# The product g of a step placed behind the selection of the step in front of it, on VectorE, in the second half of the first MLP layer

## The chip, the core and the metric

The kernel runs on one core of a Trainium2 chip. The metric is the device time of one execution in microseconds (us). Three runs of the kernel before took 456.14, 456.65 and 458.29 us; the median is 456.65. The profile was taken in one further execution of 458.42 us, whose instructions span 456.7 us.

## What is computed

Three things in a row, on 1536 tokens (2 batches of 768): a gated linear attention with 8 heads of 40 columns, then two MLP layers of 320 -> 2048 -> 320. Only the first layer is touched. Cut to what matters:

```python
def _moe_ref(x, w_in, w_out):          # first layer
    h = x @ w_in                       # (1536, 320) @ (320, 2048)
    g = h - np.tanh(h)
    return (g @ w_out).astype(np.float32)
def _moe2_ref(x, w_in, w_out):         # second layer
    h = x @ w_in
    sp = np.where(h > 20.0, h, np.log1p(np.exp(np.minimum(h, 20.0))))
    return ((h * np.tanh(sp)) @ w_out).astype(np.float32)
```

## The kernel before

The weights of a layer come in NF = 16 chunks of 128 hidden columns. Numbers are carried in two parts, a rounded high part and the rest, so that TensorE multiplies high by high, high by low and low by high.

**Steps.** The first layer cuts the tokens into NB = 6 blocks of 256. A step is one block with NP = 2 chunks. Each block is visited twice: a first pass over its first chunks (8 for block 0, 10 for the others; `CUT`), and a second pass over the rest. All first passes come first: steps 0 to 28. Then the second passes: steps 29 to 32 for block 0, and three steps for each further block, up to step 47. The last block's first pass begins with step 24. From step 48 on it is the second layer, one chunk with 512 tokens to a step.

**One step.** `mm1(i)` makes h in PSUM: 16 matmuls of 256 columns (line 579). `tile1(i)` makes g = h - tanh(h) so that it stays exact near zero, by a product and a selection:

```python
nc.scalar.activation(out=u, in_=h, func=AF.Tanh, scale=G_B)            # L601 ACT
nc.scalar.activation(out=t, in_=h, func=AF.Tanh)                       # L602 ACT
squared[:] = [nc.scalar.activation(out=u, in_=u, func=AF.Square, ...)] # L603 ACT
mark[:] = [nc.vector.tensor_tensor(g, in0=u, in1=h, op=ALU.mult)]      # L606 DVE, the product
nc.vector.tensor_tensor(t, in0=h, in1=t, op=ALU.subtract)              # L607 DVE, the difference
relus[i] = nc.scalar.activation(out=u, in_=u, func=AF.Relu, ...)       # L608 ACT, the mask
nc.vector.copy_predicated(out=g, mask=u.bitcast(U32), data=t)          # L610 DVE, the selection
```

`split_g` rounds g to gh on ScalarE (L590) and takes the rest gl on GpSimd (L591). `mm2`, LAG = 2 steps behind in the program's text, adds gh and gl times the output weights to two accumulators in PSUM (L642 to L644, 12 matmuls of 320 columns). After a block's last step VectorE adds the two accumulators into xo, four instructions (L659).

**What limits a step's start.** h has three PSUM buffers, so the matmuls of step i + 3 wait until step i's last reader of h is done, which is the difference L607. u, t and g have two buffers each. The accumulators have two, one pair of tiles at a time: a block's first L642 waits for the L659 of the block in front.

**What else these engines do there.** Weights of the second layer are converted a chunk at a time: DVE L202, ACT L210, DVE L214, ACT L217, DVE L220 and L221, six chunks in steps 29 to 47. The second layer's transposed input is made from finished blocks: PE L288, ACT L290, DVE L293.

**What sets the order.** The program is recorded with a scheduler that plays it through on a timeline and puts each engine's instructions in the order in which they come up there; the engines then run their lists strictly in that order and wait at semaphores. `after([x])` adds an edge behind x for instructions of x's own engine: it sets the order in the list and no semaphore. Since the scheduler plays the whole program, one such edge can move instructions on other engines as well.

Of the kernel before, what the change touches and what calls it, by code (L numbers as in the profile page):

```python
# [10 lines left out]
U32 = mybir.dt.uint32  # L11
# [14 lines left out]
def kernel(  # L26
# [11 lines left out]
    nc = tc.nc  # L38
# [19 lines left out]
    NP = 2  # L58
# [22 lines left out]
    NB = len(blocks1)  # L81
# [47 lines left out]

    texp, tbl, dls, squared = [], [], [], []  # L130

    scored, gated, rounded, relus, slots = {}, {}, {}, {}, {}

    spq, cvd, hold = [], [], []

# [8 lines left out]
    def after(x):  # L144
        e = ExitStack()
        for i in x:
            e.enter_context(tc.issue_after(i.ins))
        return e
# [409 lines left out]
    segs = [(bi, 0, CUT[bi]) for bi in range(NB)] + [(bi, CUT[bi], NF) for bi in range(NB)]  # L558
    tiles = [(0, bi, f) for bi, f0, f1 in segs for f in range(f0, f1, NP)]
    half = len(tiles)  # L560
    tiles += [(1, bi, f) for s in supers for f in range(NF) for bi in s]
    hps, gs, accs = {}, {}, {}

    def span(i):
        l, bi, f = tiles[i]
        return l, bi, range(f, f + (1 if l else NP)), len(blk[l, bi]) * L
# [21 lines left out]
    def split_g(i, g, n):  # L588
        gh, gl = (gp.tile([P, MX], F32R, tag=t, name=t)[:, 0:n] for t in ("gh", "gl"))
        rounded[i] = nc.scalar.activation(out=gh, in_=g, func=AF.Copy)  # L590
        nc.gpsimd.tensor_tensor(gl, in0=g, in1=gh.bitcast(F32), op=ALU.subtract)  # L591
        gs[i] = (gh, gl)

    def tile1(i):
        l, bi, fs, nt = span(i)
        n = len(fs) * nt
        h = hps.pop(i)
        u, t, g = (g2.tile([P, MX], F32, tag=nm, name=nm)[:, 0:n] for nm in "utg")

        with after([scaled[0, fs[-1] + 1]] if i < CUT[0] // NP - 1 else []):  # L600
            nc.scalar.activation(out=u, in_=h, func=AF.Tanh, scale=G_B)  # L601
            nc.scalar.activation(out=t, in_=h, func=AF.Tanh)  # L602
        squared[:] = [nc.scalar.activation(out=u, in_=u, func=AF.Square, scale=G_SA)]  # L603
        joint = i == CUT[0] // NP - 1
        with after([gated[NP]] if joint else []):
            mark[:] = [nc.vector.tensor_tensor(g, in0=u, in1=h, op=ALU.mult)]  # L606
        nc.vector.tensor_tensor(t, in0=h, in1=t, op=ALU.subtract)  # L607
        relus[i] = nc.scalar.activation(out=u, in_=u, func=AF.Relu, bias=bias[:, 0:1])  # L608
        with after([gated[NP + 1]] if joint else []):
            nc.vector.copy_predicated(out=g, mask=u.bitcast(U32), data=t)  # L610
        split_g(i, g, n)


# [62 lines left out]
    def program():  # L676
# [183 lines left out]
        for i in range(len(tiles)):  # L860
# [29 lines left out]
            if l == 0:  # L890
                tile1(i)
                if 1 < i < 4:
                    session(2 * i - 3, 2 * i - 1 + (i > 2), i == 3, [cvd[0], relus[2]] if i < 3 else [rounded[2]] * 3)
                qm.append(i)
                if len(qm) > LAG:
                    mm2(qm.pop(0))
                if i:
                    ahead(min(int(14 * (k + (i - i0 + 1) / n_seg + 0.4)), (8, 14)[i - 1] if i < 3 else 14 * NB))
                if k >= T2:
                    next(sg, None)  # L900
                    next(sg, None)
            else:
                tile2(i)
                qm.append(i)
                if len(qm) > LAG2:
                    mm2(qm.pop(0))
                next(sg, None)
# [66 lines left out]
```

## Time and profile before

| | before |
|---|---|
| median of 3 runs | 456.65 us |
| profiled execution, its own time | 458.42 us |
| its span (first to last instruction) | 456.7 us |
| PE busy | 439.7 us (96%) |
| DVE, ACT, POOL busy | 295.4, 284.2, 98.7 us |
| granted TensorE clock, mean | 1.000 |

How to read it: PE is TensorE, DVE VectorE, ACT ScalarE, POOL GpSimd. PE is busy nearly all the time, so the time of the kernel is the sum of PE's work and of the stretches in which PE stands. Matmuls overlap their neighbours in the profile (a row of 0.31 us is followed by the next after 0.15), so the distance from start to start tells more than the busy time. In a timeline row the square brackets give the time that the engine stood idle before it, and what it waited for. Steps can be found in the timeline by counting L606: step 24 is at 179.31 us, step 47 at 275.11.

### The profile page before, as it was taken

How to read it: one execution, taken by the hardware profiler on the slowest of the kernel's cores; microseconds unless marked ns; L12 is line 12 of the kernel's file. 1: busy time of each engine (PE TensorE's matmuls, PEld its weight loads, DVE VectorE, ACT ScalarE, POOL GpSimd, SP SyncE). 2: the span in 40 equal slices, each digit the busy share in tenths (PEclk: the TensorE clock that was granted, in tenths of full speed). 3: DMA queues.
4: the chain of work that ended last, by engine and by line, in shares of the span. 5: the costliest groups of instructions: out<-in, count | busy, mean ns of one | idle time of the engine just before them, and what ended most of it. 6: DMA issues, size and time to landing. Idle time of an engine off the chain costs nothing.

```text
span 456.7 us, 7966 instructions
## 1 busy us (share of the span) xinstructions
PE 439.7 (96%) x3116; PEld 399.4 (87%) x3116; DVE 295.4 (65%) x520; ACT 284.2 (62%) x519; POOL 98.7 (22%) x103
## 2 busy tenths in 40 slices
PE   9899999899999999999988899999999999999997
PEld 5657889899899999999987888998889899889996
DVE  7899999977989985566775865986922212211112
ACT  6687996584866858988687767675643332322331
POOL 2307153353442521433242232000000000000000
PEclk9999999999999999999999999999999999999999
DMA  8985526222343210001111120343110000010001
GB/s 253 377 297 184 173 76 217 76 99 69 100 161 104 65 65 1 0 17 50 63 65 65 63 64 1 86 166 130 63 59 0 1 1 1 11 48 0 1 0 57
DMA packets 22728, 38.03 MB, mean 83 GB/s; under 512 B 1348, under 2 KB 17028, under 8 KB 22692
## 3 DMA queue, kind: packets, MB, share of 16 engines
q1 hardware_dynamic: 22692, 37.54, 25.2%
q8 instruction: 24, 0.39, 0.3%
q14 instruction: 12, 0.10, 0.1%
HBM read 35.41 MB, written 1.97 MB: 82 GB/s over the span
## 4 chain that ended last, share of the span: by engine, by line
PE 52%; DVE 20%; issue 12%; ACT 7%; POOL 5%; DMA 3%; POOLq 0%; ACTq 0%; DVEq 0%; SPq 0%
PE h L579 22%; PE acc L644 7%; PE acc L642 7%; PE acc L643 7%; POOL gl L591 5%; DMA raw<-in_w_dram 3%; DVE g L606 3%; PE pv L409 2%; DVE t L607 2%; DVE raw L214 2%; DVE w L220 2%; PE sc L385 2%; PE w_ps L683 2%; DVE g L610 2%; DVE raw L202 2%
## 5 line engine op out<-in xcount | busy, mean ns | idle before, releaser
L579 PE MATMUL h<-xT,w 128*128 128x256 f32 (+1 forms) x1152 | 203.7, 321 | 6.5 <-DVE t L607 4.7
L579 PEld LDWEIGHTS h<-xT,w 128*128 128x128 f32 x1152 | 166.6, 188 | 22.9 <-PE acc L644 2.4
L642 PE MATMUL acc<-w,gh 128*128 128x320 f32 x384 | 119.3, 313 | 0.3 <-ACT xo L662 0.2
L643 PE MATMUL acc<-w,gh 128*128 128x320 f32 x384 | 118.4, 310 | 0.0
L644 PE MATMUL acc<-w,gl 128*128 128x320 f32 x384 | 113.5, 312 | 1.6 <-POOL gl L591 1.6
L591 POOL TENSOR_TENSOR gl<-g,gh 128x512 fp32r<-128x512 f32 x48 | 64.7, 1348 | 141.3 <-ACT gh L590 134.9
L623 DVE TENSOR_TENSOR gl<-g,gh 128x512 fp32r<-128x512 f32 x48 | 33.1, 690 | 82.5 <-ACT g L622 82.4
L621 ACT ACTIVATE gh<-h 128x512 fp32r<-128x512 f32 x48 | 28.8, 599 | 78.4 <-PE h L579 76.8
L642 PEld LDWEIGHTS acc<-w,gh 128*128 128x128 f32 x384 | 72.2, 188 | 3.0 <-ACT gh L590 0.5
L643 PEld LDWEIGHTS acc<-w,gh 128*128 128x128 f32 x384 | 72.2, 188 | 2.2
L644 PEld LDWEIGHTS acc<-w,gl 128*128 128x128 f32 x384 | 70.4, 188 | 4.0 <-POOL gl L591 2.9
L606 DVE TENSOR_TENSOR g<-u,h 128x512 f32<-128x512 f32 x48 | 32.8, 683 | 32.5 <-POOL gl L591 14.9
L608 ACT ACTIVATE u<-u,bias 128x512 f32<-128x512 f32 x48 | 34.8, 727 | 16.4 <-DVE g L606 16.3
L590 ACT ACTIVATE gh<-g 128x512 fp32r<-128x512 f32 x48 | 30.5, 634 | 20.0 <-DVE g L610 19.9
L610 DVE COPY_PREDICATED g<-u,t 128x512 f32<-128x512 uint32 x48 | 36.3, 780 | 2.4 <-ACT u L608 2.3
L217 ACT ACTIVATE w<-raw 128x704 fp32r<-128x704 f32 x32 | 27.3, 859 | 14.6 <-DVE raw L214 14.4
L607 DVE TENSOR_TENSOR t<-h,t 128x512 f32<-128x512 f32 x48 | 32.7, 682 | 0.0
L601 ACT ACTIVATE u<-h 128x512 f32<-128x512 f32 x48 | 28.4, 592 | 4.6 <-PE h L579 4.6
L214 DVE SCALAR_TENSOR_TENSOR raw<-raw 128x704 uint32<-128x704 uint32 x32 | 30.8, 966 | 0.7 <-ACT raw L207 0.3
L603 ACT ACTIVATE u<-u 128x512 f32<-128x512 f32 x48 | 30.3, 644 | 0.0
L602 ACT ACTIVATE t<-h 128x512 f32<-128x512 f32 x48 | 28.7, 598 | 0.0
L622 ACT ACTIVATE g<-h 128x512 f32<-128x512 f32 x48 | 28.5, 594 | 0.0
(106 smaller groups left out, 436.2 us busy)
## 6 DMA issues: line engine op xcount, KB each, us to landing
raw<-in_w_dram SPq DMA_DIRECT2D x32, 704.0 KB
qk_t<-in_qk_dram SPq DMA_DIRECT2D x12, 512.0 KB
kv_t<-in_kv_dram SPq DMA_DIRECT2D x12, 324.0 KB
out_dram<-xo SPq DMA_DIRECT2D x12, 160.0 KB
xo<-in_og_dram SPq DMA_DIRECT2D x2, 800.0 KB
xo<-in_og_dram SPq DMA_DIRECT2D x1, 320.0 KB
sd<-nr SPq DMA_DIRECT2D x20, 4.0 KB
md<-nr SPq DMA_DIRECT2D x10, 8.0 KB
```

Of the source, the lines that this page charges most:

```text
L214: third[layer, f] = nc.vector.scalar_tensor_tensor(z, in0=z, scalar=3, in1=lo32, op0=ALU.logical_shift_left, op1=ALU.bitwise_or)
L579: y = nc.tensor.matmul(t[:, k * nt:(k + 1) * nt], lhsT=w[:, o:o + P], rhs=x[:, kk, :], start=(n == 0), stop=(n == len(pairs) - 1),)
L590: rounded[i] = nc.scalar.activation(out=gh, in_=g, func=AF.Copy)
L591: nc.gpsimd.tensor_tensor(gl, in0=g, in1=gh.bitcast(F32), op=ALU.subtract)
L606: mark[:] = [nc.vector.tensor_tensor(g, in0=u, in1=h, op=ALU.mult)]
L607: nc.vector.tensor_tensor(t, in0=h, in1=t, op=ALU.subtract)
L608: relus[i] = nc.scalar.activation(out=u, in_=u, func=AF.Relu, bias=bias[:, 0:1])
L610: nc.vector.copy_predicated(out=g, mask=u.bitcast(U32), data=t)
L623: mark.append(nc.vector.tensor_tensor(gl, in0=g, in1=gh.bitcast(F32), op=ALU.subtract))
L642: turn(lambda: nc.tensor.matmul(a, lhsT=gh[:, sl], rhs=wh, start=(f in ends_), stop=False))
L643: turn(lambda: nc.tensor.matmul(a, lhsT=gh[:, sl], rhs=wl, start=False, stop=False))
L644: turn(lambda: nc.tensor.matmul(a, lhsT=gl[:, sl], rhs=wh, start=False, stop=end))
```

## The change

`chosen[i]` keeps the selection of step i. For every step after `STEADY` = 24 (steps 25 to 47) the product L606 gets an edge behind the selection of the step in front. Both are on VectorE. No instruction is added or taken away, and no semaphore.

```diff
-    scored, gated, rounded, relus, slots = {}, {}, {}, {}, {}
+    scored, gated, rounded, relus, slots, chosen = {}, {}, {}, {}, {}, {}
...
+    STEADY = tiles.index((0, NB - 1, 0))
...
-        with after([gated[NP]] if joint else []):
+        with after([gated[NP]] if joint else [chosen[i - 1]] if i > STEADY else []):
             mark[:] = [nc.vector.tensor_tensor(g, in0=u, in1=h, op=ALU.mult)]
...
-            nc.vector.copy_predicated(out=g, mask=u.bitcast(U32), data=t)
+            chosen[i] = nc.vector.copy_predicated(out=g, mask=u.bitcast(U32), data=t)
```

Lines behind the new one have numbers one higher in the kernel after: L606 is L607 there, and so on.

VectorE, before, from the product of step 41 to the difference of step 43 (raw and w are weights of the second layer):

```order
340 L606 TENSOR_TENSOR g<-u,h 128x512
341 L607 TENSOR_TENSOR t<-h,t 128x512
342 L202 TENSOR_SCALAR raw<-raw 128x704
343 L606 TENSOR_TENSOR g<-u,h 128x512
344 L607 TENSOR_TENSOR t<-h,t 128x512
345 L610 COPY_PREDICATED g<-u,t 128x512
346 L214 SCALAR_TENSOR_TENSOR raw<-raw 128x704
347 L610 COPY_PREDICATED g<-u,t 128x512
348 L220 TENSOR_TENSOR w<-raw,w 128x576
349 L221 TENSOR_TENSOR w<-raw,w 64x128
350 L606 TENSOR_TENSOR g<-u,h 128x512
351 L607 TENSOR_TENSOR t<-h,t 128x512
```

VectorE, after, from the product of step 41 to the difference of step 43:

```order
349 L607 TENSOR_TENSOR g<-u,h 128x512
350 L608 TENSOR_TENSOR t<-h,t 128x512
351 L202 TENSOR_SCALAR raw<-raw 128x704
352 L214 SCALAR_TENSOR_TENSOR raw<-raw 128x704
353 L611 COPY_PREDICATED g<-u,t 128x512
354 L607 TENSOR_TENSOR g<-u,h 128x512
355 L608 TENSOR_TENSOR t<-h,t 128x512
356 L220 TENSOR_TENSOR w<-raw,w 128x576
357 L221 TENSOR_TENSOR w<-raw,w 64x128
358 L611 COPY_PREDICATED g<-u,t 128x512
359 L607 TENSOR_TENSOR g<-u,h 128x512
360 L608 TENSOR_TENSOR t<-h,t 128x512
```

Two steps went through together before (two products, then two selections); now one step's selection is followed by the next step's product, and L220 and L221, which stood in front of a pair's first product, stand behind a difference and in front of a selection.

ScalarE, before, from the squares of steps 41 and 42 on (L608 masks, L590 rounding, L601 and L602 the tanh of step 43, L217 the rounding of a weight chunk):

```order
319 L603 ACTIVATE u<-u 128x512 x2
320 L608 ACTIVATE u<-u,bias 128x512 x2
321 L590 ACTIVATE gh<-g 128x512
322 L601 ACTIVATE u<-h 128x512
323 L602 ACTIVATE t<-h 128x512
324 L217 ACTIVATE w<-raw 128x704
325 L603 ACTIVATE u<-u 128x512
326 L590 ACTIVATE gh<-g 128x512
```

ScalarE, after, from the mask of step 41 on:

```order
331 L609 ACTIVATE u<-u,bias 128x512
332 L604 ACTIVATE u<-u 128x512
333 L217 ACTIVATE w<-raw 128x704
334 L591 ACTIVATE gh<-g 128x512
335 L602 ACTIVATE u<-h 128x512
336 L603 ACTIVATE t<-h 128x512
337 L609 ACTIVATE u<-u,bias 128x512
338 L604 ACTIVATE u<-u 128x512
```

ScalarE's list repeats with one step now: mask, square of the next step, (a weight chunk,) rounding, the two tanh of the step after that. L217 stood behind the tanh of the pair and in front of its square, and now stands between a square and a rounding.

PE, before, the matmuls for h of steps 34 and 35 and the first six accumulating ones of step 31 (one row is one matmul where no count stands):

```order
627 L579 MATMUL h<-xT,w 128x256 x32
628 L642 MATMUL acc<-w,gh 128x320
629 L643 MATMUL acc<-w,gh 128x320
630 L642 MATMUL acc<-w,gh 128x320
631 L643 MATMUL acc<-w,gh 128x320
632 L644 MATMUL acc<-w,gl 128x320 x2
```

PE, after, from the rest of step 35's matmuls on, with eleven of step 32's accumulating matmuls and the first six of step 36:

```order
645 L580 MATMUL h<-xT,w 128x256 x9
646 L643 MATMUL acc<-w,gh 128x320
647 L644 MATMUL acc<-w,gh 128x320
648 L643 MATMUL acc<-w,gh 128x320
649 L644 MATMUL acc<-w,gh 128x320
650 L580 MATMUL h<-xT,w 128x256 x6
651 L645 MATMUL acc<-w,gl 128x320 x2
652 L643 MATMUL acc<-w,gh 128x320
653 L644 MATMUL acc<-w,gh 128x320
654 L645 MATMUL acc<-w,gl 128x320
655 L643 MATMUL acc<-w,gh 128x320
656 L644 MATMUL acc<-w,gh 128x320
```

Before, 32 matmuls of two steps alternate with 24 accumulating ones; now the two kinds alternate step by step, and some of the next step's h are put between the gh and the gl part of a step. POOL's and SP's lists keep their order.

## Rows read from the trace of the kernel before

**Rows 1.** Busy us of each engine by stretch of us, with instructions and TensorE's clock
```profile
199.00:217.00 18.00, 18.00 (x139) 18.00 (x139) 11.89 (x21) 14.98 (x29) 5.60 (x4) 1.00 0.13 41
225.00:252.00 27.00, 23.43 (x173) 22.00 (x172) 19.06 (x38) 20.21 (x36) 8.25 (x6) 1.00 0.17 55
```

**Rows 2.** Groups by line on PE, 225.1 to 282: busy, mean ns | idle, releaser
```profile
L579 PE MATMUL h<-xT,w 128*128 128x256 f32 x160 | 20.8, 284 | 4.2 <-DVE t L607 4.2
...
L644 PE MATMUL acc<-w,gl 128*128 128x320 f32 x53 | 15.0, 317 | 1.0 <-POOL gl L591 1.0
```

**Rows 3.** Timeline of PE: start, us, engine line, xcount [idle before]
```profile
202.69 3.89 PE L579 MATMUL h<-xT,w 128*128 128x256 f32 x32
...
217.22 3.91 PE L579 MATMUL h<-xT,w 128*128 128x256 f32 x32
220.96 0.82 PE L288 MATMUL xt<-ident,xo 128*128 128x128 f32 x6
221.54 0.39 PE L642 MATMUL acc<-w,gh 128*128 128x320 f32 x1
...
259.91 2.15 PE L579 MATMUL h<-xT,w 128*128 128x256 f32 x16 [0.95 <-DVE t L607]
...
269.10 3.82 PE L579 MATMUL h<-xT,w 128*128 128x512 f32 x16
...
277.44 2.01 PE L579 MATMUL h<-xT,w 128*128 128x512 f32 x8
```

**Rows 4.** Timeline of DVE in front of the PE wait at 259.91
```profile
257.38 0.76 DVE L220 TENSOR_TENSOR w<-raw,w 128x576 fp32r<-128x576 f32 x1 [1.03 <-ACT w L217]
...
258.48 0.69 DVE L606 TENSOR_TENSOR g<-u,h 128x512 f32<-128x512 f32 x1
259.08 0.69 DVE L607 TENSOR_TENSOR t<-h,t 128x512 f32<-128x512 f32 x1
```

**Rows 5.** Timeline of ACT: one wait for h, one L217, and steps 46 and 47
```profile
197.50 0.60 ACT L601 ACTIVATE u<-h 128x512 f32<-128x512 f32 x1 [0.26 <-PE h L579]
...
256.50 0.85 ACT L217 ACTIVATE w<-raw 128x704 fp32r<-128x704 f32 x1
...
272.36 0.63 ACT L590 ACTIVATE gh<-g 128x512 fp32r<-128x512 f32 x1 [1.68 <-DVE g L610]
272.90 0.58 ACT L601 ACTIVATE u<-h 128x512 f32<-128x512 f32 x1
273.38 0.59 ACT L602 ACTIVATE t<-h 128x512 f32<-128x512 f32 x1
...
274.37 0.63 ACT L603 ACTIVATE u<-u 128x512 f32<-128x512 f32 x1
275.83 0.72 ACT L608 ACTIVATE u<-u,bias 128x512 f32<-128x512 f32 x1 [0.82 <-DVE g L606]
277.46 0.63 ACT L590 ACTIVATE gh<-g 128x512 fp32r<-128x512 f32 x1 [0.91 <-DVE g L610]
```

**Rows 6.** Timeline of DVE, step 47, which goes through alone
```profile
275.11 0.69 DVE L606 TENSOR_TENSOR g<-u,h 128x512 f32<-128x512 f32 x1 [2.22 <-ACT u L603]
275.71 0.68 DVE L607 TENSOR_TENSOR t<-h,t 128x512 f32<-128x512 f32 x1
276.58 0.76 DVE L610 COPY_PREDICATED g<-u,t 128x512 f32<-128x512 uint32 x1 [0.19 <-ACT u L608]
```

**Rows 7.** Timeline of POOL, step 47
```profile
278.17 1.29 POOL L591 TENSOR_TENSOR gl<-g,gh 128x512 fp32r<-128x512 f32 x1 [2.31 <-ACT gh L590]
```

**Rows 8.** Timeline of DVE: the same small instruction twice, beside POOL and alone
```profile
166.67 0.84 DVE L419 TENSOR_TENSOR den<-hv,den 128x8 f32<-128x8 f32 x1
...
169.20 0.16 DVE L419 TENSOR_TENSOR den<-hv,den 128x8 f32<-128x8 f32 x1
```

**Rows 9.** Timeline around the second layer's start: DVE's last drain, PE's wait
```profile
280.81 0.62 DVE L659 SCALAR_TENSOR_TENSOR xo<-acc,xo 128x256 f32<-128x256 f32 x2 [3.46 <-PE acc L644]
...
319.83 1.20 PE L579 MATMUL h<-xT,w 128*128 128x512 f32 x4 [1.07 <-DVE w L220]
```

## The prediction

> **What bounds the kernel now.** I read the busy time by stretches first. From 199 to 217 us PE is busy all 18.00 us; from 225 to 252 it is busy 23.43 of 27.00 us, and in both the granted clock is 1.00, the level of 2.4 GHz [rows 1]. So PE's work sets the time, and PE has holes in the second passes. The groups by line, for 225 to 282 us, say what ends them: 4.2 us before L579, released by the difference L607, and 1.0 us before L644, released by POOL's gl [rows 2]. Both are the step's own chain over ACT, DVE and POOL, which runs too late for PE.
>
> The marked idle is less than what PE loses, since a matmul's row ends after the next could have started. I take the loss from starts. Without a wait, steps 32 to 35 take 217.22 - 202.69 = 14.53 us, 3.63 a step [rows 3]. From 217.22 to 269.10 there are steps 36 to 47, twelve of them: 51.88 us, against 12 x 3.63 = 43.6 and two sets of transposes at 221.54 - 220.96 = 0.58 each. That leaves 7.1 us. From 269.10 to 277.44 there are 16 matmuls of 512 columns (3.82 us) and 24 accumulating ones (two steps less 32 matmuls for h, 7.27 - 3.89 = 3.38): 7.2 of 8.3 us, which leaves 1.1. PE loses 8.2 us in this stretch, 5.2 of them marked.
>
> Why the chain is late can be read at one hole. PE's step 46 waits 0.95 us at 259.91 [rows 3] for the difference of step 43, which ran at 259.08; its product ran at 258.48, behind L220 of a weight chunk, which had itself stood 1.03 us for ACT's L217 [rows 4]. L217 ran at 256.50 [rows 5], behind the tanh of a step that nobody needed yet. That is the paired list: two steps through each engine together, with the chunk's work in front of the pair.
>
> **The change part by part.** Nothing is added or removed, so no engine's work changes; POOL's and SP's lists are the same. What moves is the lists of DVE, ACT and PE, from pairs to single steps, and the whole question is whether the new ring of one step is shorter than PE's 3.63 us, and how much of PE's need it leaves as slack.
>
> *The ring.* With the edge, the product of step k+1 stands behind the selection of step k, which needs the mask of step k on ACT. Step 47 goes through alone and shows the links: mask 275.83 to selection 276.58 is 0.75, selection to rounding 277.46 is 0.88 [rows 5, 6]. Then rounding to tanh is 0.54 and tanh to tanh 0.48 (272.36, 272.90, 273.38), and 0.48 more to the next mask [rows 5]. Sum 3.13 us. In the 1.63 us between mask and rounding ACT has the next square to do: 0.72 + 0.63 = 1.35 fits. DVE puts product (0.60 to the next start) and difference (0.68) behind the selection (0.76): 0.75 + 0.76 + 0.60 + 0.68 = 2.79, inside 3.13. A weight chunk's piece on ACT, L217 at 0.85, makes 2.20 of the 1.63: 0.57 more, a ring of 3.70. Two steps of three have such a piece (L210, which I price as L217): 3.13 + 3.70 + 3.70 = 10.5 against PE's 10.9. So ACT's ring is faster than PE, though not by much, and it can catch up.
>
> *The buffer of h.* From the end of step k's matmuls: 0.26 to its first tanh [rows 5], 0.48, 0.48, then the mask of k-1, 0.75 to its selection, 0.76, product 0.60, difference 0.68: 4.0 us, and 0.15 to PE (259.08 + 0.69 to 259.91, less what is rounding) [rows 3, 4]. PE wants that buffer for step k+3, whose matmuls have to start 3 x 3.63 less their own 1.95 and the 1.1 of the accumulating ones put between them: 7.8 us after. Slack 3.6.
>
> *gl.* From the end of step k+1's matmuls the selection of k starts after 0.26 + 0.48 + 0.48 + 0.75 = 1.97, its rounding 0.88 later, POOL 0.71 later (277.46 to 278.17), done after 1.29 [rows 5, 7]: 4.9. PE's list puts gl of k behind all of step k+3 and a part of k+4, some 8 us after. Slack 3.
>
> *The tightest place.* In the new list the first drain of a block (L659) stands between a difference and the next selection, so DVE waits there for PE. After step 34's matmuls PE has 22 for h and 24 accumulating ones until the block's last: 22 x 0.122 + 24 x 0.141 = 6.1 us (0.122 is 3.89 / 32, 0.141 is 3.38 / 24). DVE reaches the drain at 4.0, stands 2.1, then drains a pair of rows (0.62 [rows 9]), selects (0.76), drains 0.62, and makes product and difference (1.28): 9.5 with the release. PE wants that difference at 6.1 + 26 x 0.122 + 16 x 0.141 + about 0.2 of transposes = 11.7. Margin 2.2: no wait, and this comes at five block ends.
>
> *Two DVE and POOL instructions at once.* The same L419 took 0.84 us beside POOL's gl and 0.16 alone [rows 8]: POOL holds DVE up. In the pairs POOL works mostly while DVE waits; in the ring it works beside DVE. By the ring's links gl of k runs from 0.88 + 0.71 = 1.59 to 2.88 after its selection, the next selection is due at 3.13, after it; but L220, due at about 2.0, would be held 0.9 and push a selection to 3.9, six times, which the slack covers. At the block ends a selection held for a whole gl (1.29) leaves 0.9 of the 2.2.
> The Trainium skill (SBUF — State Buffer, "Who interferes with whom") says that a DVE instruction with two SBUF inputs and a GpSimd instruction that reads SBUF exclude each other, and the first holds the pair to its end; the selection and L220 have two, product and difference, which read h from PSUM, one. L419 agrees with it (two inputs, 0.84 against 0.16). It speaks against the change, but by it the sum stays, and the margin at the block ends falls as said.
>
> *The second layer.* PE waits 1.07 us at 319.83 for L220 [rows 9], at the end of a chain of weight chunks that starts behind DVE's last drain, for which DVE stood 3.46 us at 280.81. In the new list two of the second layer's gl and two L202 stand in front of that drain, so the chunks start earlier against PE. It is worth between -1.3 (the wait goes, with its refill) and +1.3 (the chain shifts the other way); I take -0.4.
>
> **The sum.** All waits of the stretch go: -8.2; second layer -0.4: -8.6 us. The profiled execution took 458.42 us, 1.7 more than its span of 456.7, so it becomes 449.8. It lies 1.8 above the median of 456.65; for a median I predict 448.0. If PE's waits for gl alone stayed it would be some 450, and if everything in the second layer went too, 447.
>
> **The rivals.**
> - *Part of it.* Where two L210 and two L290 come in one step, the ring is longer than 3.70 by two pieces, about 1.7 us, and PE's slack is spent once for each of the two places; with the six chunks on top, some 4 us of waits stay: 452.5. For it: ACT's ring is 10.5 of 10.9. Against: 3.6 us of slack. 15%.
> - *Given back in the second layer.* Between the drain at 280.81 and the wait at 319.83 weight chunks are loaded and converted one after the other. If the loads set that stretch, PE comes 8 us earlier to the same chunk: 456 to 457. For it: the wait at 319.83. Against: the chain starts at DVE behind PE's last accumulating matmul [rows 9], so it moves along. 13%.
> - *Slower.* The drains stand before a selection at five block ends. The margin is 2.2 us; when it is gone (a gl held 1.29, L217's 0.57 and a late gl of the draining block together), PE waits for a difference behind a drain that waits for PE, and each time the stand of 2.1 and 0.62 for the drain put in between come on top: 5 x 2.7 = 13.6, less 8.2: 462. For it: the stand is new, since before, the drains stood behind both differences of a pair. Against: all three must fall together. 9%.
> - *The change does nothing.* The list of after is different in three engines, so this is out.
>
> **How the numbers follow.** Forecast 63%, with its own range 446.3 to 450.5; part 15%; given back 13%; slower 9%. Faster by over 0.5% (under 454.4; a measurement of this kernel tells no less from no change) is forecast and part: 0.78. Same 0.13, slower 0.09. The range from 446.2 to 455.5 leaves out the slower case, most of the third and the forecast's lower tail.
>
> **What the profile after would show.** Right: DVE's rows read selection, product, difference, one step after the other; from 225 to 282 us PE's groups L579 and L644 have almost no idle; steps 36 to 47 start every 3.63 us beside transposes; the first 512-column matmuls start near 262 instead of 269.10; DVE stands some 2 us before a first drain and PE doesn't follow. Wrong: idle on PE before L579 released by the difference right behind a drain (slower), ACT's L601 following L590 without a gap over many steps while PE waits (part), or matmuls of 512 columns waiting for L220 or for loads by as much as the first layer gained (given back).

## The result and the profile after

The kernel after took 448.86 us (median of 6 runs, 448.56 to 451.22), the kernel before 456.69 (6 runs beside it, 456.14 to 458.29). The ratio is 0.983, 95% interval 0.9804 to 0.9856: 7.8 us less. Forecast were 448.0 and 8.6 less.

The profiled execution of after took 451.22 us with a span of 449.5. It is 2.4 above the median for a reason outside the change: in the attention, between 51 and 60 us, where the lists of both kernels are still the same, TensorE's granted clock lay at 0.62 on the mean, part of it at the level of 1.2 GHz; the profile of before had 1.000 throughout. From 44 to 51 us PE was busy 6.61 us in after and 6.68 in before, both at 1.00, the level of 2.4 GHz, so what made the clock fall stays open.

```profile
51.00:60.00 9.00, 9.00 (x73) 8.54 (x71) 6.47 (x16) 6.61 (x13) 1.37 (x1) 0.62 0.39 128
```

The same hole, which no edge touches, stands at 185.73 us in before and at 187.87 in after, so 2.14 us are to be taken off later times of after before they are compared.

The page of after, busy time and shares of the chain of waits:

```profile
PE 440.2 (98%) x3116; PEld 402.4 (90%) x3116; DVE 304.6 (68%) x520; ACT 284.1 (63%) x519; POOL 97.5 (22%) x103
...
PE 82%; DVE 10%; ACT 4%; issue 2%; POOL 1%; DVEq 0%; ACTq 0%; POOLq 0%
```

Busy time of each engine by stretch, after (PE, PEld, DVE, ACT, POOL, clock, DMA share, GB/s), which answers to [rows 1]:

```profile
199.00:217.00 18.00, 18.00 (x140) 18.00 (x139) 16.06 (x22) 16.31 (x32) 7.19 (x5) 1.00 0.13 42
225.00:252.00 27.00, 27.00 (x212) 26.99 (x211) 26.43 (x43) 24.31 (x44) 9.07 (x7) 1.00 0.17 55
```

PE is busy all 27.00 us where it was busy 23.43. VectorE is busy 26.43 of them; it was 19.06. The groups on PE from 225.1 to 274 us, against [rows 2]:

```profile
L580 PE MATMUL h<-xT,w 128*128 128x256 f32 (+1 forms) x184 | 28.2, 296 | 0.0
...
L645 PE MATMUL acc<-w,gl 128*128 128x320 f32 x53 | 14.7, 309 | 0.0
```

Neither 4.2 nor 1.0 is left. I also count holes from starts: distances over 0.3 us between neighbouring matmuls, less 0.15 each. From the first matmul of step 25 to the first of 512 columns they add up to 6.2 us in before and 0.4 in after (this is the count in all that follows; short gaps fall out of it, so it is less than the 8.2 of the prediction). Timeline of PE, after, against [rows 3]:

```profile
203.66 1.10 PE L580 MATMUL h<-xT,w 128*128 128x256 f32 x8
...
263.25 2.02 PE L580 MATMUL h<-xT,w 128*128 128x512 f32 x8
...
269.31 2.00 PE L580 MATMUL h<-xT,w 128*128 128x512 f32 x8
```

The first matmul of 512 columns starts at 263.25, or 261.1 with the 2.14 off: 8.0 earlier than 269.10. Eight of the accumulating matmuls have moved behind it (264 instead of 272 lie in front of it since step 25), so I check at the first matmul of step 54, in front of which both kernels have done the same matmuls since step 25, which starts at 177.18 in before and at 179.32 in after. Timeline of PE, before and then after:

```profile
294.32 1.09 PE L579 MATMUL h<-xT,w 128*128 128x512 f32 x4
```

```profile
288.47 1.78 PE L580 MATMUL h<-xT,w 128*128 128x512 f32 x7
```

117.14 us in before and 109.15 in after: again 8.0. From there to the end of the span it is 162.4 and 161.0, 1.4 less. Of the three rows further up, the other two are the first matmuls of steps 32 and 50, which take the h buffers of steps 29 and 47. Timeline of VectorE, after, the difference of step 29 and then from step 44 on:

```profile
200.00 0.68 DVE L608 TENSOR_TENSOR t<-h,t 128x512 f32<-128x512 f32 x1
...
257.90 0.87 DVE L202 TENSOR_SCALAR raw<-raw 128x704 uint32<-128x704 uint32 x1
258.81 0.89 DVE L214 SCALAR_TENSOR_TENSOR raw<-raw 128x704 uint32<-128x704 uint32 x1
259.62 0.78 DVE L611 COPY_PREDICATED g<-u,t 128x512 f32<-128x512 uint32 x1
260.28 0.67 DVE L607 TENSOR_TENSOR g<-u,h 128x512 f32<-128x512 f32 x1
260.87 0.68 DVE L608 TENSOR_TENSOR t<-h,t 128x512 f32<-128x512 f32 x1
261.47 1.64 DVE L220 TENSOR_TENSOR w<-raw,w 128x576 fp32r<-128x576 f32 x1
263.12 0.29 DVE L221 TENSOR_TENSOR w<-raw,w 64x128 fp32r<-64x128 f32 x1
263.44 0.76 DVE L611 COPY_PREDICATED g<-u,t 128x512 f32<-128x512 uint32 x1
...
266.56 0.77 DVE L611 COPY_PREDICATED g<-u,t 128x512 f32<-128x512 uint32 x1 [1.20 <-ACT u L609]
267.22 0.60 DVE L660 SCALAR_TENSOR_TENSOR xo<-acc,xo 128x256 f32<-128x256 f32 x2
267.75 0.67 DVE L607 TENSOR_TENSOR g<-u,h 128x512 f32<-128x512 f32 x1
268.34 0.68 DVE L608 TENSOR_TENSOR t<-h,t 128x512 f32<-128x512 f32 x1
268.94 0.61 DVE L660 SCALAR_TENSOR_TENSOR xo<-acc,xo 128x256 f32<-128x256 f32 x2
```

Selection, product, difference alternate, as the edge wants. Two things to read here. First, the *room*: the end of a difference to the start of the matmuls that take its h buffer. It is 203.66 - 200.68 = 3.0 us at step 29 and 269.31 - 269.02 = 0.3 at step 47. Nothing waits, but it has been shrinking. Second, VectorE never waits for PE in front of a drain L660; it waits for ScalarE's mask.

And L220 takes 1.64 us where it took 0.76 [rows 4]. POOL's gl beside it:

```profile
261.20 1.29 POOL L592 TENSOR_TENSOR gl<-g,gh 128x512 fp32r<-128x512 f32 x1 [2.81 <-ACT gh L591]
```

gl ends at 262.49; L220 ends at 263.11, 0.62 after it.

### The profile page after: what moved, and what is told of

Same layout as the page of the kernel before. It is cut to its first block, busy times and chain, and to the rows that moved or that the text cites. A ratio compares the mean times of both kernels' runs of the same rounds, so it can differ in the third digit from the quotient of the medians.

```text
span 449.5 us, 7966 instructions
## 1 busy us (share of the span) xinstructions
PE 440.2 (98%) x3116; PEld 402.4 (90%) x3116; DVE 304.6 (68%) x520; ACT 284.1 (63%) x519; POOL 97.5 (22%) x103
## 4 chain that ended last, share of the span: by engine, by line
PE 82%; DVE 10%; ACT 4%; issue 2%; POOL 1%; DVEq 0%; ACTq 0%; POOLq 0%
PE h L580 37%; PE acc L645 11%; PE acc L643 11%; PE acc L644 11%; PE pv L409 3%; PE w_ps L684 2%; PE sc L385 2%; PE xt L288 1%; DVE g L611 1%; PE it L396 1%; DVE raw L214 1%; DVE g L607 1%; DVE Dm L389 1%; ACT raw L210 1%; POOL gl L592 1%
## 5 line engine op out<-in xcount | busy, mean ns | idle before, releaser
L580 PE MATMUL h<-xT,w 128*128 128x256 f32 (+1 forms) x1152 | 206.6, 321 | 1.3 <-DVE t L608 0.5
L580 PEld LDWEIGHTS h<-xT,w 128*128 128x128 f32 x1152 | 169.2, 189 | 16.7 <-issue 0.9
L645 PE MATMUL acc<-w,gl 128*128 128x320 f32 x384 | 114.8, 312 | 0.6 <-POOL gl L592 0.6
L592 POOL TENSOR_TENSOR gl<-g,gh 128x512 fp32r<-128x512 f32 x48 | 63.6, 1324 | 133.1 <-ACT gh L591 131.3
L645 PEld LDWEIGHTS acc<-w,gl 128*128 128x128 f32 x384 | 70.8, 189 | 1.5 <-POOL gl L592 0.9
L611 DVE COPY_PREDICATED g<-u,t 128x512 f32<-128x512 uint32 x48 | 39.0, 815 | 11.3 <-ACT u L609 11.0
L607 DVE TENSOR_TENSOR g<-u,h 128x512 f32<-128x512 f32 x48 | 32.6, 679 | 12.6 <-POOL gl L592 4.6
L217 ACT ACTIVATE w<-raw 128x704 fp32r<-128x704 f32 x32 | 27.2, 857 | 12.3 <-DVE raw L214 12.1
L608 DVE TENSOR_TENSOR t<-h,t 128x512 f32<-128x512 f32 x48 | 32.8, 683 | 0.0
L602 ACT ACTIVATE u<-h 128x512 f32<-128x512 f32 x48 | 28.2, 588 | 5.1 <-PE h L580 5.1
L214 DVE SCALAR_TENSOR_TENSOR raw<-raw 128x704 uint32<-128x704 uint32 x32 | 30.8, 968 | 0.9 <-ACT raw L207 0.4
L220 DVE TENSOR_TENSOR w<-raw,w 128x576 fp32r<-128x576 f32 x31 | 29.8, 960 | 1.6 <-ACT w L217 1.3
```

The costliest lines, as they stand in the source:

```text
L214: third[layer, f] = nc.vector.scalar_tensor_tensor(z, in0=z, scalar=3, in1=lo32, op0=ALU.logical_shift_left, op1=ALU.bitwise_or)
L580: y = nc.tensor.matmul(t[:, k * nt:(k + 1) * nt], lhsT=w[:, o:o + P], rhs=x[:, kk, :], start=(n == 0), stop=(n == len(pairs) - 1),)
L611: chosen[i] = nc.vector.copy_predicated(out=g, mask=u.bitcast(U32), data=t)
L645: turn(lambda: nc.tensor.matmul(a, lhsT=gl[:, sl], rhs=wh, start=False, stop=end))
```

## The experiments

Two measures stand beside the times: holes from step 25 to the first matmul of 512 columns (before 6.2, after 0.4), and the room of h. An edit also lets the scheduler move neighbours a place or two; what matters of that is told. Intervals are 95%, against the kernel before.

**The pair or the chunks? `pairs_two_chunks`.** To keep pairs whatever else is edited, the selection of a pair's first step is recorded behind the second step's difference; with this alone the lists of all engines are those of before, row for row, so before is its control.

```diff
+        def pick(behind=()):
+            with after(behind):
+                nc.vector.copy_predicated(out=g, mask=u.bitcast(U32), data=t)
+            split_g(i, g, n)
+        if 25 <= i < 47 and i % 2:
+            picked[i] = pick
+            return
+        if i - 1 in picked:
+            picked.pop(i - 1)(diffs[i])
+        pick()
...
-        CY, R2, E2 = 6, 3, 6
+        CY, R2, E2 = 6, 3, 2
```

> The list of before, held in pairs of steps by edges, but only two of the six weight chunks of the second layer are converted in the second passes; the other four follow in the second layer. Theory (chunk work in front of a pair's product makes the holes; pairs alone are fast enough, since between steps 26 and 30 of before, where pairs run without a chunk, the room of h grew from 2.5 to 4.1 us): from step 36 on there is no chunk work and PE's holes go; idle before the matmuls for h between 225 us and the end of the first layer under 1 us of the 4.2, time 449 to 451. Rival (two steps handed through together are too slow for three buffers of h by themselves): more than half of the idle stays, 453 to 456.

471.03 us, ratio 1.0315 (1.029 to 1.034): the second layer pays for the four chunks that it now converts itself (10.1 us of PE's marked idle there stand before its accumulating matmuls, for ScalarE's gh). In the stretch in question the theory's sign is there: holes 1.1, and before the matmuls for h 0.2 us of idle are left of 4.2. So with little chunk work pairs nearly keep up with PE. The time forecast for the whole was wrong by 20 us, since I had not priced the second layer.

**The other corner, `singles_two_chunks`.** The kernel before with `E2 = 2` and nothing else; the scheduler then goes to single steps by itself.

> Only two of the six weight chunks are converted in the second passes, and the steps go through singly from step 23 on. Beside the run with two chunks in pairs (86.65 us from the first matmul of step 25 to the first of 512 columns) it shows what pairs cost without the chunks. If the pair costs time by itself: 83.6 to 84.2 us here, as in the kernel after with six chunks. If two chunks in pairs had lost only through something else in the stretch: 86 and more. The second layer loses as much as in that run, some 18 us, so the whole takes 466 to 468.

475.66 us in its one run, which gives no verdict on the time; PE waits 16.9 us in the second layer for L217, where the same four chunks are missing, and the granted clock falls four times there (0.50 from 280 to 283 us, for one). The stretch: holes 0.0, room 1.8 to 5.8 at all steps from 26 to 46. The four corners of holes are then pairs with six chunks 6.2, pairs with two 1.1, singles with six 0.4, singles with two 0.0. By the sign on record, from the first matmul of step 25 to the first of 512 columns, it is 84.59 us here and 86.65 in pairs, with the same matmuls in between: pairs cost 2.1 us even with two chunks, which the holes show only in part. Most of the loss takes pairs *and* chunks.

**The chunk's place within pairs, `pairs_c_behind` and `pairs_l217_c_behind`.** L220 and L221 behind a difference instead of in front of a product; in the second run L217 also behind the pair's square. Core of the edit, on top of the held pairs:

```diff
+        for low in ready:                  # one chunk's last instructions, a step later
+            low(diffs[i], squared)         # (first run: without squared)
```

> The list of before in pairs; only L220 and L221 of each chunk move from in front of a pair's product to behind a difference of the pair. If VectorE's list alone is the cause: holes go, 449 to 451. If ScalarE's L217, which still stands in front of a pair's square, holds the product as much as L220 does (at the hole of 259.91 the product of step 43 could start only 0.4 us earlier without L220: L217 ends near 257.3, square 0.63, product 258.0 instead of 258.48): six holes shrink by some 0.4 each, 453 to 455. I take the second, 454.

> As the run before, and ScalarE's L217 of each chunk also moves, from in front of a pair's square to behind it; still pairs. Theory (place of the chunk's work on both engines makes the holes, not the pair): 449 to 451.5, idle before the matmuls for h under 1.5 us of the 4.2. Rival (the pair itself): 453 to 456.

457.91 us, ratio 1.0031 (1.0018 to 1.0044), and 458.74, 1.0048 (1.0031 to 1.0065): both a little slower than before, holes 6.0 in both. My theory that the chunk's place in front of the product makes the holes fell. The groups on PE, 217 to 269 us, show why. Before:

```profile
L579 PE MATMUL h<-xT,w 128*128 128x256 f32 x192 | 24.7, 283 | 4.2 <-DVE t L607 4.2
...
L644 PE MATMUL acc<-w,gl 128*128 128x320 f32 x49 | 13.8, 315 | 0.5 <-POOL gl L591 0.5
```

With L220 and L221 behind a difference:

```profile
L586 PE MATMUL h<-xT,w 128*128 128x256 f32 x192 | 25.0, 284 | 1.0 <-DVE t L617 0.8
L664 PE MATMUL acc<-w,gh 128*128 128x320 f32 x48 | 15.2, 319 | 0.4 <-ACT gh L597 0.4
...
L666 PE MATMUL acc<-w,gl 128*128 128x320 f32 x47 | 13.5, 322 | 2.5 <-POOL gl L598 2.5
```

The difference does come earlier (4.2 to 1.0), but the selection behind the chunk comes later, and with it gh and gl: 0.5 becomes 2.9 (0.4 before the gh part, 2.5 before the gl part). In a pair the work of a chunk delays one end or the other.

**Is POOL's gl the link? `pairs_no_read`.** The list of before held in pairs, and:

```diff
-        nc.gpsimd.tensor_tensor(gl, in0=g, in1=gh.bitcast(F32), op=ALU.subtract)
+        nc.gpsimd.memset(gl.bitcast(F32), 0.0)             # from step 25 on
```

> The list of before, held in pairs by edges, and POOL writes zeros into gl from step 25 on and reads nothing (that part is left out), so that gl no longer stands between a rounding and the product that takes the same buffer of g. In before VectorE's products stand 5.9 us for gl between 199 and 270 us. If the ring of pairs is long because ScalarE and VectorE wait for each other, gl being only the last of the links: 454 to 457. If gl is the link that makes pairs slow: 449 to 451.

449.63 us, ratio 0.9844 (0.9815 to 0.9872), holes 0.4: pairs with all six chunks and PE has no hole but the one at 185 us. g has two buffers, so the product of step k + 2 waits until gl of step k has read g; a pair's two gl stand one behind the other on POOL (1.41 us each on the mean from 199 to 268 us), between rounding and the next product. VectorE's groups, 199 to 268 us, before and then with the memset:

```profile
L606 DVE TENSOR_TENSOR g<-u,h 128x512 f32<-128x512 f32 x16 | 10.9, 684 | 13.3 <-POOL gl L591 5.9 <-ACT u L603 4.7 <-issue 2.4
```

```profile
L611 DVE TENSOR_TENSOR g<-u,h 128x512 f32<-128x512 f32 x18 | 12.3, 685 | 8.7 <-ACT u L608 8.5
```

The product's wait for gl is gone. But ScalarE's list changed as well in this run (at most pairs a step's square now stands directly behind its own tanh, where both squares stood behind both), some chunks stand at another place in the pair, and the memset is shorter than the subtraction (0.53 us). So how much is the link and how much the rest stays open. That POOL slowed VectorE down in pairs is no rival: L220 took 0.74 to 0.76 us at each chunk of before. The kernel after shows the same wait gone without a memset, by order alone (same view, after):

```profile
L607 DVE TENSOR_TENSOR g<-u,h 128x512 f32<-128x512 f32 x19 | 12.8, 675 | 0.2 <-issue 0.2
```

**The chunk's place within single steps, `singles_c_front`.**

```diff
-        ... else [chosen[i - 1]] if i > STEADY else []):
+        ... else [chosen[i - 1]] + list(lows.values())[-1:] if i > STEADY else []):
```

> The kernel after (single steps), but L220 and L221 of each chunk are put back in front of a product, directly behind the selection, where VectorE must wait for L217. Theory (the place of the chunk's work counts): VectorE stands some 0.9 us at each of six chunks and the difference comes 1.0 to 1.9 us later, more than the room of 0.3 to 1.7 us that the differences of after have at steps 43 to 47: part of the holes comes back, 451 to 453. Rival (single steps are enough, wherever the chunk stands): 448.5 to 449.5.

452.51 us, ratio 0.9909 (0.9887 to 0.9932), holes 2.1, room 0.2 or less at nine of the steps 30 to 46. Nearly half of the gain is gone, within the forecast. In single steps the place does count. The reason that I gave is only a small part of it: VectorE stands 1.2 us for L217 over all six chunks and not 0.9 at each. L220 and L221 themselves, L221 held to 958 ns on the mean, now lie in front of a product. VectorE's groups, 199 to 268 us:

```profile
L221 DVE TENSOR_TENSOR w<-raw,w 64x128 fp32r<-64x128 f32 x6 | 5.8, 958 | 0.1
...
L220 DVE TENSOR_TENSOR w<-raw,w 128x576 fp32r<-128x576 f32 x6 | 4.6, 759 | 1.2 <-ACT w L217 1.2
```

**From which step is the edge needed? `edge_from_34`.** `i > STEADY + 9` instead of `i > STEADY`.

> The kernel after with the edge only for steps 34 to 47; steps 25 to 32 stay in pairs, single steps begin with step 33. Theory (only the second passes from some 217 us on lose time): from the first matmul of step 25 to the first of 512 columns 84 to 84.5 us as in the kernel after (83.93; before 91.93), time within 0.6 of after: 448.5 to 449.5. Rival (the lead that single steps build up in steps 25 to 33 is needed): h has only 1.1 to 1.5 us of room at steps 33 and 34 of before, so PE loses 1 to 3 us, 450 to 452.

451.31 us, ratio 0.9878 (0.9846 to 0.991); holes 2.5, and 86.6 us from step 25 to the first 512 columns instead of 83.9. My theory fell, the rival is right. PE's waits, timeline:

```profile
220.28 0.41 PE L643 MATMUL acc<-w,gh 128*128 128x320 f32 x1 [0.77 <-ACT gh L591]
...
232.22 2.12 PE L580 MATMUL h<-xT,w 128*128 128x256 f32 x16 [0.43 <-DVE t L608]
...
244.33 0.95 PE L580 MATMUL h<-xT,w 128*128 128x256 f32 x6 [0.30 <-DVE t L608]
```

Single steps that begin with 1.5 us of room do not win any back; they run at 0.1 to 2.0 to the end. The other way round, the edge for steps 25 to 33 alone was not run, since it gives all engines the same lists as after, row for row: once in single steps the scheduler stays there.

**Why is the lead needed? `gl_no_read` and `late_no_read`.** The kernel after, and `edge_from_34`, with the memset of above for gl.

> The kernel after, but from step 25 on POOL writes zeros into gl instead of g less gh (that part of the computation is left out), so it reads nothing from SBUF. If POOL's reads hold VectorE: L220 takes 0.75 us everywhere instead of 1.63 to 1.67, the selection never over 0.8, VectorE's busy time between 225 and 252 us falls by 2 to 4 of 26.4. If POOL's writes are enough to hold it: L220 stays near 1.6. The time: by the theory that the held time is covered, 448.4 to 449.4; by the rival that it costs PE time, 446 to 448.

> The edge only from step 34 on, as in the run with that name, and POOL writes zeros into gl from step 25 on and reads nothing (that part of the computation is left out). If the lead from steps 25 to 33 is needed only because the held VectorE makes the ring of single steps no faster than PE: the ring is faster here, the holes of that run (1.0, 0.4, 0.7 and 0.6 us from start to start after 219 us) shrink to one or none, 448.4 to 449.6. If the lead is needed anyway: 450.5 to 451.5 as there.

448.70 us, ratio 0.9808 (0.9784 to 0.9833), and 448.82, 0.9812 (0.979 to 0.9835); holes 0.4 in both. VectorE by stretch and L220, `gl_no_read`:

```profile
225.00:252.00 27.00, 27.00 (x212) 26.99 (x211) 23.00 (x45) 24.31 (x45) 3.69 (x7) 1.00 0.24 82
...
L220 DVE TENSOR_TENSOR w<-raw,w 128x576 fp32r<-128x576 f32 x6 | 4.5, 751 | 0.0
```

3.4 us of VectorE's 26.43 were not work but being held by POOL's gl. With that time back the room is 4.1 us at step 47 instead of 0.3, and a start at step 34 makes no hole. Whether the ring or PE is ahead shows where ScalarE's first tanh stands idle for h. Groups from 199 to 261 us, after and then `gl_no_read`:

```profile
L602 ACT ACTIVATE u<-h 128x512 f32<-128x512 f32 x16 | 9.3, 581 | 0.0
```

```profile
L605 ACT ACTIVATE u<-h 128x512 f32<-128x512 f32 x16 | 9.6, 598 | 5.9 <-PE h L580 5.9
```

The ring of after never waits for PE in this stretch; without the held time it is ahead and waits. Since no product of after waits for gl in this stretch, the memset takes away the holding there and not a link. In `late_no_read` it does both (products of `edge_from_34` still stand 3.5 us for gl from 199 to 268 us), so that run doesn't divide the two. For the time of the kernel after the held time costs nothing that can be seen: 448.70 against 448.86.

**Which engine sets the ring? `dve_plus` and `act_plus`.** One more small instruction in each of steps 25 to 47.

```diff
+                padded = [nc.vector.memset(pad, 0.0)]          # dve_plus, 128x256, before the selection
+                padded = [nc.scalar.activation(out=pad, in_=zeros, func=AF.Copy)]   # act_plus, 128x128, before the rounding
```

> The kernel after with one more instruction on VectorE in each of steps 25 to 47, between a difference and the selection: a memset of 128x256 into an unused tile, about 0.3 us by the length of the drains of that size. If VectorE is the engine that the ring of single steps is full on (98% busy from 225 to 252 us, room for h down from 3.0 us at step 29 to 0.3 at step 47): 23 x 0.3 = 7 us more, of which the room takes 2 to 3: PE waits, 452 to 455. If ScalarE sets the ring, as predicted (10.5 of 10.9 us per three steps, 3.6 us of room): 449 to 450.

> The kernel after with one more instruction on ScalarE in each of steps 25 to 47, between the mask and the rounding: a copy of 128x128 into an unused tile, about 0.3 us. If VectorE is full and ScalarE waits for its selection there (0.4 to 1.1 us at most steps of after): the piece lies in that wait, 448.5 to 450. If ScalarE sets the ring, as predicted: 10.5 + 0.9 = 11.4 of 10.9 us per three steps, 0.5 us too much seven times, 3.6 us of which the room takes part: 450 to 452.5.

448.50 us, ratio 0.9812 (0.9789 to 0.9835), and 449.46, 0.9835 (0.9811 to 0.986); holes 0.4 and 0.6. Both theories of one full engine fell. VectorE: 23 times 0.27 us are free, and the room at step 47 is 2.5, more than in after. The groups of `dve_plus`, 199 to 270 us:

```profile
L221 DVE TENSOR_TENSOR w<-raw,w 128x576 fp32r<-128x576 f32 x6 | 7.0, 1163 | 0.2 <-ACT w L218 0.2
...
L613 DVE MEMSET pad<- 128x256 f32 x18 | 4.9, 272 | 0.0
```

The chunk's larger subtraction (L221 in this kernel) takes 1163 ns on the mean where it took 1565 in after: part of the memsets' time is time in which it would have been held. ScalarE: 23 times 0.31 us are 7.1, and PE loses 0.5 of them (84.4 us from step 25 to the first 512 columns instead of 83.9); the forecast for ScalarE setting the ring, 450 to 452.5, was missed. The differences of steps 29 and 45, `act_plus` and then `dve_plus`:

```profile
198.00 0.68 DVE L609 TENSOR_TENSOR t<-h,t 128x512 f32<-128x512 f32 x1
...
259.73 0.69 DVE L609 TENSOR_TENSOR t<-h,t 128x512 f32<-128x512 f32 x1
```

```profile
197.19 0.69 DVE L609 TENSOR_TENSOR t<-h,t 128x512 f32<-128x512 f32 x1
...
257.76 0.71 DVE L609 TENSOR_TENSOR t<-h,t 128x512 f32<-128x512 f32 x1
```

From end to end that is 3.86 and 3.79 us a step, against 3.80 in after (200.68 to 261.55). An engine that set the ring alone would have made it some 0.3 longer. So neither does; each waits for the other in turn, and the time in which VectorE is held is the one part that a run has taken out. ScalarE is the nearer bound: its copies eat the room down to 0.1 at steps 40, 43 and 46, and make 0.2 us of hole.

**The second layer, `drains_first`.**

```diff
+        with after([drains[-3]] if i == half else drains[-1:] if i == half + 1 else []):
+            mark.append(nc.vector.tensor_tensor(gl, ...))
```

> The kernel after, its first layer unchanged; at the start of the second layer the first two gl and L202 stand behind VectorE's last drains again, as in the kernel before. Theory (order: in after the weight chunks start earlier because they stand in front of the drains): PE's wait for L220 in the second layer comes back with 0.8 to 1.3 us, 449.7 to 450.2. Rival (the wait went because the first layer lost its waits, so that the loads of the chunks have no part of it): no wait, 448.5 to 449.2.

450.04 us, ratio 0.9836 (0.9808 to 0.9863); by time it can't be told from after. PE's one wait of the second layer is back, of 0.55 us:

```profile
311.44 1.20 PE L581 MATMUL h<-xT,w 128*128 128x512 f32 x4 [0.55 <-DVE w L220]
```

After has 0.0 there. So the order at the layer's start does decide whether PE waits; the size is half of the 1.07 of before, and what took the other half isn't shown.

Little is left to win in the stretch: PE has 0.4 us of holes there.

## Why the prediction was right, and where it was not

*The bound and the loss.* Right. PE lost some 8 us in the second passes and gets 8.0 back. The sum said 8.6; medians give 7.8. The two profiled executions differ by 7.2, and by 9.3 when the 2.14 of the early clock are taken off after; of that 8.0 lie ahead of step 54 and 1.4 behind. The profile of before was itself 1.8 above its median, and no trace shows where. The second layer gave 1.0 more than I took and the medians give 1.5 less than the traces; the two pull apart, so that 448.0 came so close to 448.86 is partly luck. One small slip: 0.122 and 0.141 us a matmul come from the length of a row. From start to start it is 0.117 and 0.147 (the accumulating ones behind 202.69 begin at 206.43); in a whole step the two errors cancel.

*The cause.* Half wrong. It is the paired list with the chunks in it, as the four corners show. But I gave the paired list "with the chunk's work in front of the pair" and took L220 and L217 in front of one product for the mechanism. Moving them within pairs gains nothing. As I now read it, the pair's ring goes mask, selection, rounding, gl, next product, two of each, with engines waiting for each other, and a chunk makes it longer wherever it stands; that gl is its decisive link is in part argued (`pairs_no_read` changed more than the link). POOL's gl stood as a link in the page of before, where I had read only PE's waits for it (of the 14.9 us, which are for the whole kernel, 5.9 lie between 199 and 268 us):

```profile
L606 DVE TENSOR_TENSOR g<-u,h 128x512 f32<-128x512 f32 x48 | 32.8, 683 | 32.5 <-POOL gl L591 14.9
```

*The ring.* The sum of links (10.5 us per three steps, 3.5 a step) came out too short. Ends of differences, step 29 to 45: (261.55 - 200.68) / 16 = 3.80 us a step in after, and 4.35 in before by the same steps; PE's own pace, starts of steps 29 to 45, is 3.72. The ring does not catch up, as I wrote; it loses about 0.1 us a step, and the 3.0 us of room at step 29 carry it to step 47 with 0.3 left. `edge_from_34` shows what that lead is worth, 2.4 us. Nor does ScalarE set it, as the sum assumed: 0.31 us more on ScalarE made a step 0.06 longer. From the end of a step's matmuls to the end of its difference I added up 4.0 us; steps 25 to 47 of after took 4.1 to 8.0. So the slack of 3.6 wasn't there each step; room of that size is what the ring has when VectorE is never held (2.4 to 5.4 in `gl_no_read` from step 26 on). That no wait came is owed to the lead, which the prediction doesn't have.

*The port.* Right on the result: held, and covered. Undersized: L220 was held by 0.88 to 0.92 five times and 0.42 once, but L202 by up to 0.91 and the selection up to 0.61 as well, 3.4 us in 27. The Trainium skill (SBUF — State Buffer, "Who interferes with whom") names more than I drew from it: a tensor_scalar can enter a two-port mode and then also contends for that pair, and a DVE instruction with two SBUF inputs does not contend with a GpSimd instruction that only writes. The traces agree: L202, a tensor_scalar, took up to 1.43 us where it takes 0.52, and in `gl_no_read` L220 at 234.91 took 0.75 beside a memset that began at 234.77.

*The tightest place.* Not seen. VectorE comes to the first drains at the five block ends 4.7 to 9.9 us behind the matmuls of the step whose difference stands last in front of them, instead of 4.0, so PE is done first and there is no stand of 2.1. For the same reason the slower rival had nothing to start from.

*The second layer.* I took -0.4 out of -1.3 to +1.3. The wait of 1.07 went whole and the stretch from step 54 to the end is 1.4 us shorter, which is at the lower end; the reason given, the new order, brings back 0.55 when it is undone.

*Signs.* Alternating rows, no idle at L580 and L645, the first 512 columns near 262: all there. Steps 36 to 47 start 3.76 us apart with the transposes between them; VectorE's stand of 2 us in front of a drain didn't come. The rivals "part" and "given back" left no sign: PE's groups from 190 us to the end show 0.0 idle each.

## What to carry to other kernels

When two steps go through a chain of engines together, look for the buffer that may tie the second step's end to the next pair's start (here the product stood 5.9 us for gl in pairs and not at all in single steps); no engine has to be faster for single steps to win. Judge such a ring by the room from step to step, not by the waits: 0.3 us and 4 us of room look alike in the idle column, and a lead built before the tight stretch may be what hides a ring that is too slow. Before a chunk of work is moved, ask what stands behind it at both ends: in pairs its place only chose who was late, in single steps the wrong place cost nearly half of the gain.

## What the runs showed of the hardware

Held time is not work, and in this kernel it gave way. VectorE was 98% busy from 225 to 252 us in after, yet took 4.9 us of memsets between 199 and 270 us without a loss (`dve_plus`); from 225 to 252 its busy time only went from 26.43 to 26.69 of 27. It works in the other direction too. POOL's gl at 212.20 started 0.02 us after VectorE's L214 and took 2.02 us instead of 1.29 (after):

```profile
212.18 0.89 DVE L214 SCALAR_TENSOR_TENSOR raw<-raw 128x704 uint32<-128x704 uint32 x1
```

```profile
212.20 2.02 POOL L592 TENSOR_TENSOR gl<-g,gh 128x512 fp32r<-128x512 f32 x1 [2.66 <-ACT gh L591]
```

And a memset on POOL, 0.53 us alone, took 0.92 when L202 had begun 0.07 us ahead of it (`gl_no_read`):

```profile
208.05 0.53 DVE L202 TENSOR_SCALAR raw<-raw 128x704 uint32<-128x704 uint32 x1
```

```profile
208.12 0.92 POOL L593 MEMSET gl<- 128x512 f32 x1 [4.97 <-PE acc L648]
```
